# Attention's second pass in one run: the order of score products and value sums on TensorE, and eight modulation rows moved to later steps

## The chip, the cores and the metric

The kernel runs on one core of a Trainium2 chip. A core has five engines that run their own instruction streams in order: TensorE (PE in the profile, PEld its weight loads), VectorE (DVE), ScalarE (ACT), GpSimd (POOL) and SyncE (SP), which here issues all the DMAs. They wait for each other through semaphores. The metric is the device time of one execution in microseconds, lower is better.

## What is computed

One transformer block on 2048 tokens of 1024 channels, in float32: an attention with 32 heads in 4 segments of 512 tokens (a causal softmax inside the segment, plus a memory `M`, `z` that is carried from segment to segment), then a token-mixing MLP. Both are modulated by six rows that come from `silu(c) @ w_mod`.

```python
mod = (_silu(c) @ w_mod).reshape(c.shape[0], 6, 1, -1)
sa, ca, ga, sb, cb, gb = (mod[:, 0], mod[:, 1], mod[:, 2], mod[:, 3], mod[:, 4], mod[:, 5])
h = _layernorm(x, axis=-1) * (1 + ca) + sa
x = x + ga * _A_ref(h, A_wq, A_wk, A_wv, A_wo, A_beta)
h = _layernorm(x, axis=-1) * (1 + cb) + sb
x = x + gb * _B_ref(h, B_w1, B_b1, B_w2, B_b2)
...
logits = jnp.einsum("bhqd,bhkd->bhqk", qs, ks) * scale + mask
p = _softmax(logits, axis=-1)
a_dot = jnp.einsum("bhqk,bhkd->bhqd", p, vs)
o = g * a_mem + (1.0 - g) * a_dot
```

The two parts of it that matter here are `p` and `p @ vs` for one head of one segment, and `ga`, the row that scales the attention's result.

## The kernel before

**Stages.** A start normalises the first segment and makes the first modulation rows. The attention follows as a loop over 128 steps, then the product with `wo` (line 791), the second norm, and the MLP (line 921, more than half of the time), which the change leaves alone.

**Steps.** The heads are handled in 8 groups of 4, the segments in two passes: the first pass does segments 0 and 1 for all 8 groups, the second segments 2 and 3. `t` (0 to 31) counts (pass, group, segment), and step `n = 4 t + h` is one head of one segment. Steps 64 to 127 are the second pass. In round `n` the loop emits `scores` of step `n`, `maxima` of step `n + 3`, `values` of step `n - 2` (`VL = 2`), `project` pieces for a later `t`, and whatever was planned for that round.

**scores** (tiles `a`, lines 515 to 523) makes the transposed logits of a head in three PSUM banks. The causal triangle leaves 512 + 384 + 384 columns. The third bank takes two products: 128 columns (line 521) and then 256 (line 522). The operands are 32-bit tiles `sk`. ACT takes the exponential of each bank into `p` (lines 516, 519, 523), POOL masks the diagonal blocks (526), ACT makes the 16-bit high part `ph` (528), and POOL the 16-bit low part `p` in two halves of 640 columns (530).

**values** (tile `pv`, line 544) makes the weighted sums of a head with 20 products: 10 with the high part as weights and 97 columns of `vp`, then 10 with the low part and 65 columns. All add up in one PSUM bank. VectorE then divides and folds them (547, 549, 551). Below, these 20 products are called the sums. **maxima** makes the row maxima (products 478, VectorE 480), **project** the keys and values (192), queries (200) and transposes (405), **memory** the products 450 and 460 with VectorE lines 452 to 454 between them and the result `am`.

**Order.** The program is written round by round, but the instructions are put into each engine's stream by a list scheduler that weighs what is ready. So the pieces of one round are mixed with those of its neighbours. `tc.issue_after(i)` keeps what is written inside it behind instruction `i`; `behind(n, engines)` does this with the instructions that `scores` or `maxima` left in `marks` for round `n`.

**Modulation rows.** The last four of the six rows of `mod` are computed late on VectorE: 32 blocks `j` of 128 columns of `w_mod`. `mod_fetch(j)` (line 569) loads a block into a `raw` buffer, of which there are three, shared with the weight parts that pass 1 fetches, the token tiles and the `wo` blocks. `mod_late(j)` (line 573) multiplies and sums it. After block 7 the row `ga` is complete, is transposed on PE and written out; round 62 reads it back into `gaw`, and the `wo` blocks are scaled by it from round 66 on.

`mx` in lines 921 and 928 is the MLP's accumulator; `wv`, `wq` are weight parts that are split into two 32-bit parts (line 122); `wsp` and `hT` are scratch in DRAM, written in pass 1 and read in pass 2.

Of the kernel before, what the change touches and what calls it, by code (L numbers as in the profile page):

```python
# [18 lines left out]
P = 128  # L19
# [8 lines left out]
NV = 97  # L28
# [3 lines left out]
VL = 2  # L32
ML0 = 36
# [8 lines left out]
def attention_and_mlp(ctx, tc, x, wq, wkv, wo, beta, w1, b1, w2, b2, c, wm_a, wm_b, out):  # L42
    nc = tc.nc
    V, A, G, T, SY = nc.vector, nc.scalar, nc.gpsimd, nc.tensor, nc.sync
# [451 lines left out]
    marks = {}  # L496

    @contextmanager
    def behind(n, engines):

        with ExitStack() as s:
            for e in engines:
                if (n, e) in marks:
                    s.enter_context(tc.issue_after(marks[n, e].ins))
            yield

    def scores(t, h):
        d = st[t]
        n = 4 * t + h
        q, k = d["sk", h][:, 0], d["sk", h][:, 1]  # L510
        p32 = r_.tile([P, 1280], F32, tag="p32", bufs=3, name=f"p32_{t}_{h}")
        hi, lo = r_.tile([P, 1280], F16, tag="ph", bufs=3, name=f"ph{t}_{h}"), p32.bitcast(F16)[:, 0:1280]
        d["ph", h] = hi, lo
        b0 = bank("s2", 2, f"a0_{t}_{h}")
        T.matmul(b0, k[:, 0:128], q, start=True, stop=True)  # L515
        A.activation(p32[:, 0:512], b0, AF.Exp, scale=SCALE, bias=shift)  # L516
        b1_ = bank("s2", 2, f"a1_{t}_{h}")
        T.matmul(b1_[:, 0:384], k[:, 128:256], q[:, 128:512], start=True, stop=True)  # L518
        A.activation(p32[:, 512:896], b1_[:, 0:384], AF.Exp, scale=SCALE, bias=shift)
        b2_ = bank("s2", 2, f"a2_{t}_{h}")  # L520
        T.matmul(b2_[:, 0:128], k[:, 384:512], q[:, 384:512], start=True, stop=True)
        T.matmul(b2_[:, 128:384], k[:, 256:384], q[:, 256:512], start=True, stop=True)  # L522
        A.activation(p32[:, 896:1280], b2_[:, 0:384], AF.Exp, scale=SCALE, bias=shift)  # L523
        for base, step in ((0, 512), (896, 128)):
            w = bass.AP(tensor=p32.tensor, offset=p32.offset + base, ap=[p32.ap[0], [step, 2], [1, 128]])
            G.affine_select(w, w, pattern=[[0, 2], [1, 128]], compare_op=ALU.is_ge, fill=0.0, base=0,  # L526
                            channel_multiplier=-1)
        marks[n, "A"] = A.copy(hi, p32)  # L528
        for c in (slice(0, 640), slice(640, 1280)):
            marks[n, "G"] = G.tensor_tensor(lo[:, c], p32[:, c], hi[:, c], op=ALU.subtract)  # L530

    def values(t, h):
        pr, g, seg = its[t]
        d = st[t]
        am, ph = d["am"], d["ph", h]
        pv = bank("pv", 1, f"pv{t}_{h}").rearrange("p (a n) -> p a n", a=4)
        col = {0: lambda i: 128 * i, 1: lambda i: 512 + 128 * (i - 1), 2: lambda i: 1024 + 128 * (i - 2),
               3: lambda i: 896}
        n = 0
        for part, w in ((0, NV), (1, 65)):  # L540
            for i in range(4):
                for j in range(i + 1):
                    o = col[j](i)
                    T.matmul(pv[:, i, 0:w], ph[part][:, o:o + 128], d["vp"][:, j, h, 0:w], start=(n == 0),  # L544
                             stop=(n == 19), skip_group_check=True)
                    n += 1
        V.reciprocal(pv[:, :, 0], pv[:, :, 0])
        red = r_.tile([P, 4, 32], F32, tag="red", bufs=2, name=f"red{t}_{h}")
        V.tensor_reduce(red, pv[:, :, 1:97].rearrange("p a (c e) -> p a e c", c=3), axis=AX.X, op=ALU.add)
        ah = am[:, :, 32 * h:32 * h + 32]  # L550
        V.scalar_tensor_tensor(red if seg else ah, red, gate[:, 1, 4 * g + h:4 * g + h + 1],
                               pv[:, :, 0:1].to_broadcast([P, 4, 32]), op0=ALU.mult, op1=ALU.mult)
        if seg:
            G.tensor_tensor(ah, ah, red, op=ALU.add)
        if h < 3:
            return
        ps = bank("ms", 1, f"ops{t}")
        for i in range(4):
            T.transpose(ps[:, 128 * i:128 * i + 128], am[:, i], ident)
        ot = r_.tile([P, L], F32, tag="ot", bufs=1, name=f"ot{t}")  # L560
        A.copy(ot, ps)
        SY.dma_start(oT[g, :, L * seg:L * seg + L], ot)
        del st[t]
# [3 lines left out]
    def mod_fetch(j):  # L567
        r = a.tile([P, D], F32, tag="raw", bufs=3, name=f"rawm{j}")
        SY.dma_start(r, wm_b[P * j:P * j + P])
        return r  # L570

    def mod_late(j, r):
        V.scalar_tensor_tensor(r, r, 1.0, scb, op0=ALU.mult, op1=ALU.mult, accum_out=mcol[:, j:j + 1])
        if j == 7:
            mod_rows(0, 8)
        if j == 31:
            V.tensor_scalar_add(mcol[:, 16:24], mcol[:, 16:24], 1.0)
            mod_rows(8, 32)
# [14 lines left out]
    def at(f, n):  # L593
        if 0 <= n < 4 * NI:
            f(n // 4, n % 4)
# [25 lines left out]
    parts = (("v", 0), ("v", 1), ("q", 0))  # L621
# [36 lines left out]
    def later(n, fetch, m, f, engines):  # L658

        got = []  # L660
        plan(n, lambda: got.append(fetch()))
        plan(m, lambda: f(got[0]), engines)
# [13 lines left out]
                  n + n1, lambda r, g=g, kind=kind, part=part: split_part(g, kind, part, r), "A")  # L676
        plan(n + 4, lambda g=g: keep_w(g))
    for j in range(32):
        n = ML0 + 2 * j + (8 if j >= 8 else 0)
        later(n, lambda j=j: mod_fetch(j), n + (2 if j < 8 else 1), lambda r, j=j: mod_late(j, r), "V")  # L680
    plan(WO0 - 3, lambda: spread(gaw, 0))
    for i in range(8):
        n = WO0 + WOS * i
# [2 lines left out]
    for n in range(-LEADS, 4 * NI + VL):  # L686
        at(scores, n)
        at(maxima, n + LEADS)
        at(values, n - VL)
        m = n + LEADP  # L690
        if 0 <= m + 4 < 4 * NI:
            t = (m + 4) // 4
            if its[t][:2] not in W:
                with tc.issue_after(last_sk[t - 2 if t > 16 else 0, 3].ins):
                    load_w(its[t][1], its[t][0])
        if m >= 8:
            at(project, m)
        if 59 <= m < 67:
            seg, ct = 2 + (m - 59) // 4, 2 * ((m - 59) % 4)
            with ExitStack() as s:  # L700
                if seg == 3:
                    s.enter_context(tc.issue_after((last_sk[15, 3] if ct < 4 else last_nt[14, 3]).ins))
                reload_h(seg, ct)
                reload_h(seg, ct + 1)
        if 4 * NI - 5 <= m < 4 * NI + 3:
            i = m - 4 * NI + 5
            for c in (2 * (i % 4), 2 * (i % 4) + 1):
                wop[c, i // 4] = new_page(f"wo{c}_{i // 4}")
                if c < 5 or i < 4:
                    SY.dma_start(wop[c, i // 4].bitcast(F32), wos[c, i // 4])  # L710
        for f, engines in todo.pop(n, ()):
            with behind(n, engines):
                f()
# [427 lines left out]
```

## Time and profile before

| | |
|---|---|
| three runs | 2225.91, 2229.25, 2231.14 us; median 2229.25 us |
| the profiled execution | 2226.6 us, of which the span from first to last instruction is 2224.9 us |
| PE | busy 2190.3 us (98%), 13786 matmuls |
| DVE, ACT, POOL | busy 1666.7, 1135.7, 725.8 us (75%, 51%, 33%) |
| TensorE clock | 0.997 of full speed in the mean |

The profile's times are those of the profiled execution, so sums are made against 2226.6 us. A PE that is 98% busy leaves little idle time to win, but "busy" counts a matmul from its start to its modelled end, and matmuls overlap. How long a product holds the engine is read from the distance between starts, in the timeline. Step 0 of the attention starts at 98 us, step 64 at 564 us, and the last sums end near 1025 us.

### The profile page before, as it was taken

Reading aid. Unit: us, or ns where it says so; the run is one execution under the profiler, and the core shown is the slowest. Engines: PE = TensorE matmul, PEld = TensorE weight load, DVE = VectorE, ACT = ScalarE, POOL = GpSimd, SP = SyncE. Lnnn points to the kernel's source line nnn. Section 1 sums busy time; section 2 is a strip of 40 time slices with the busy share of each in tenths; the row PEclk is TensorE's granted clock in tenths of the full one; section 3 lists DMA queues with packets and bytes.
Section 4 is the critical chain, followed back from the end, with each engine's and each line's share of the span. In section 5 each row is a group of like instructions: output and inputs, shape, how many; then the busy total and the mean of one; then the engine's idle time right before and its main releaser. Section 6 shows DMA issues by size and latency. Waiting matters only on the chain.

```text
span 2224.9 us, 38052 instructions
## 1 busy us (share of the span) xinstructions
PE 2190.3 (98%) x13786; PEld 1881.0 (85%) x13786; DVE 1666.7 (75%) x3762; ACT 1135.7 (51%) x2050; POOL 725.8 (33%) x831
## 2 busy tenths in 40 slices
PE   8999999999999999999999999999999999999999
PEld 5988898888999999888888888888888888888887
DVE  7676777756777777664858766888888886969687
ACT  5486776756666666654636533533334242424232
POOL 2175766646767776663002200033330000000000
PEclk9999999999999999999999999999999999999999
DMA  7666666686556666664754687655556542414134
GB/s 287 192 187 191 175 181 193 189 279 216 170 180 205 188 183 211 193 219 143 231 194 186 226 304 275 243 223 220 204 202 219 206 148 64 145 57 147 57 123 151
DMA packets 175183, 423.03 MB, mean 190 GB/s; under 512 B 17524, under 2 KB 71828, under 8 KB 166036
## 3 DMA queue, kind: packets, MB, share of 16 engines
q1 hardware_dynamic: 174996, 420.61, 57.5%
q8 instruction: 109, 1.79, 0.3%
q14 instruction: 78, 0.64, 0.1%
HBM read 244.62 MB, written 125.06 MB: 166 GB/s over the span
## 4 chain that ended last, share of the span: by engine, by line
PE 87%; DVE 5%; DMA 3%; ACT 2%; POOL 1%; issue 1%; SPq 0%; DVEq 0%; ACTq 0%
PE mx L921 48%; PE nps L192 11%; PE po L791 8%; PE qps L200 7%; PE pv L544 3%; PE a L515 1%; PE sz L478 1%; PE sx L478 1%; DMA sk<-nt 1%; PE up L460 1%; PE a L518 1%; POOL p L530 1%; PE a L522 1%; PE sy L478 1%; PE rd L450 1%
## 5 line engine op out<-in xcount | busy, mean ns | idle before, releaser
L921 PE MATMUL mx<-bU,sp 128*128 128x512 f32 x2352 | 534.3, 389 | 0.9 <-DVE ac L928 0.9
L921 PEld LDWEIGHTS mx<-bU,sp 128*128 128x128 f32 x2352 | 441.3, 188 | 93.4 <-issue 1.3
L119 ACT CAST sp<-wr 128x384 fp32r<-128x384 f32 (+2 forms) x408 | 218.1, 547 | 431.8 <-PE mx L921 349.1
L192 PE MATMUL nps<-wv,h 128*128 128x256 f32 x3072 | 431.2, 283 | 1.6 <-DVE h L122 0.7
L921 PE MATMUL mx<-bA,sp 128*128 128x512 f32 x1764 | 430.5, 389 | 0.0
L530 POOL TENSOR_TENSOR p<-p,ph 128x640 f16<-128x640 f32 x256 | 380.2, 1485 | 138.5 <-ACT ph L528 134.5
L192 PEld LDWEIGHTS nps<-wv,h 128*128 128x128 f32 x3072 | 400.3, 189 | 9.4 <-DVE h L122 2.0
L921 PEld LDWEIGHTS mx<-bA,sp 128*128 128x128 f32 x1764 | 331.2, 188 | 68.7
L122 DVE TENSOR_TENSOR sp<-wr,sp 128x384 fp32r<-128x384 f32 (+2 forms) x408 | 259.8, 648 | 24.7 <-ACT sp L119 24.4
L928 DVE TENSOR_TENSOR ac<-mx,ac 128x512 f32<-128x512 f32 x280 | 189.9, 687 | 85.2 <-PE mx L921 84.1
L200 PE MATMUL qps<-h,wq 128*128 128x512 f32 x768 | 197.9, 400 | 0.0
L528 ACT CAST ph<-p 128x1280 f16<-128x1280 f32 x128 | 161.4, 1261 | 59.7 <-POOL p L526 59.6
L791 PE MATMUL po<-wo,ots 128*128 128x512 f32 x768 | 180.9, 391 | 0.0
L791 PEld LDWEIGHTS po<-wo,ots 128*128 128x128 f32 x768 | 142.7, 188 | 28.7
L200 PEld LDWEIGHTS qps<-h,wq 128*128 128x128 f32 x768 | 141.6, 190 | 27.7
L921 PE MATMUL mx<-bB,sp 128*128 128x512 f32 x588 | 164.0, 389 | 0.0
L526 POOL TENSOR_SCALAR_AFFINE_SELECT p<-p 128x256 f32<-128x256 f32 x256 | 134.1, 529 | 81.8 <-ACT p L523 53.9
L921 PEld LDWEIGHTS mx<-bB,sp 128*128 128x128 f32 x588 | 110.4, 188 | 22.9
L480 DVE CUSTOM_DVE_ANT_0 sz<-sz,mask 128x512 f32<-128x512 f32 x128 | 89.1, 696 | 52.0 <-PE sz L478 49.5
L480 DVE CUSTOM_DVE_ANT_0 sx<-sx,mask 128x128 f32<-128x128 f32 (+1 forms) x256 | 93.7, 366 | 44.1 <-PE sx L478 37.9
L928 DVE TENSOR_TENSOR cc<-mx,cc 128x512 f32<-128x512 f32 x140 | 94.9, 684 | 37.6 <-PE mx L921 37.4
L516 ACT ACTIVATE p<-a,shift 128x512 f32<-128x512 f32 x128 | 88.4, 691 | 41.2 <-PE a L515 40.4
(209 smaller groups left out, 3244.7 us busy)
## 6 DMA issues: line engine op xcount, KB each, us to landing
sk<-sg SPq DMA_DIRECT2D x384, 128.0 KB
wr<-in_w_dram SPq DMA_DIRECT2D x28, 1024.0 KB
wr<-in_w_dram SPq DMA_DIRECT2D x32, 768.0 KB
bstu<-ucd SPq DMA_DIRECT2D x28, 768.0 KB
wsp<-wv SPq DMA_DIRECT2D x32, 512.0 KB
rawm<-in_wm_b_dram SPq DMA_DIRECT2D x32, 512.0 KB
wv<-wsp SPq DMA_DIRECT2D x32, 512.0 KB
pcd<-cc SPq DMA_DIRECT2D x14, 1024.0 KB
```

The costliest lines, as they stand in the source:

```text
L119: last_hi[0] = A.copy(hi, src)
L122: return lo_eng.tensor_tensor(lo, src, hi.bitcast(F32), op=ALU.subtract)
L192: T.matmul(ps[:, aa], h[:, j, 128 * tt:128 * tt + 128], wt[:, i, o:o + 256], start=(n == 0), stop=(n >= 6 * NK - 2), skip_group_check=True)
L200: T.matmul(ps, wt[:, i, o:o + 128], h[:, j], start=(k + n == 0), stop=(3 * k + n == 3 * NK - 1))
L480: marks[4 * t + h - LEADS, "V"] = V.tensor_tensor_reduce(o, o, mask[:, 384 - 128 * i:], 1.0, -3.0e38, op0=ALU.add, op1=ALU.max, accum_out= ...
L516: A.activation(p32[:, 0:512], b0, AF.Exp, scale=SCALE, bias=shift)
L526: G.affine_select(w, w, pattern=[[0, 2], [1, 128]], compare_op=ALU.is_ge, fill=0.0, base=0, channel_multiplier=-1)
L528: marks[n, "A"] = A.copy(hi, p32)
L530: marks[n, "G"] = G.tensor_tensor(lo[:, c], p32[:, c], hi[:, c], op=ALU.subtract)
L791: T.matmul(ps, os_[:, i, P * ct:P * ct + P], wop[ct, nh][:, j], start=(n == 0), stop=(n == 3 * NK - 1))
L921: T.matmul(ps, ops[q][:, i, P * k:P * k + P], b[:, j], start=(m == 0 and first), stop=(m == 3 * nk - 1), skip_group_check=True)
L928: V.tensor_tensor(d, ps, d, op=ALU.add)
```

## The change

Four edits. In `scores` the third bank's two products change places, 256 columns first, and both now set `marks[n, "P"]`, so the mark is the 128-column one. In `values`, in the second pass only, the sums run in reverse: the low part first, and in each part the last block of rows first. In the loop, for steps of the second pass, `values` of step `n - 2` stands behind the mark of step `n`, so behind the last score product of that round. The first eight modulation blocks are fetched in rounds 49 to 56 and used one round later; before, they were fetched in rounds 36, 38, ... 50 and used two rounds later. Blocks 8 to 31 keep their rounds.

```diff
         b2_ = bank("s2", 2, f"a2_{t}_{h}")
-        T.matmul(b2_[:, 0:128], k[:, 384:512], q[:, 384:512], start=True, stop=True)
-        T.matmul(b2_[:, 128:384], k[:, 256:384], q[:, 256:512], start=True, stop=True)
+        for lo_, hi_, kt in ((128, 384, 2), (0, 128, 3)):
+            marks[n, "P"] = T.matmul(b2_[:, lo_:hi_], k[:, 128 * kt:128 * kt + 128], q[:, 128 * kt:], start=True,
+                                     stop=True)
         A.activation(p32[:, 896:1280], b2_[:, 0:384], AF.Exp, scale=SCALE, bias=shift)
...
-        for part, w in ((0, NV), (1, 65)):
-            for i in range(4):
-                for j in range(i + 1):
-                    o = col[j](i)
-                    T.matmul(pv[:, i, 0:w], ph[part][:, o:o + 128], d["vp"][:, j, h, 0:w], start=(n == 0),
-                             stop=(n == 19), skip_group_check=True)
-                    n += 1
+        order = [(i, j) for i in range(4) for j in range(i + 1)]
+        parts = [(0, NV), (1, 65)]
+        if pr:
+            order.reverse()
+            parts.reverse()
+        for part, w in parts:
+            for i, j in order:
+                o = col[j](i)
+                T.matmul(pv[:, i, 0:w], ph[part][:, o:o + 128], d["vp"][:, j, h, 0:w], start=(n == 0),
+                         stop=(n == 19), skip_group_check=True)
+                n += 1
...
     for j in range(32):
-        n = ML0 + 2 * j + (8 if j >= 8 else 0)
-        later(n, lambda j=j: mod_fetch(j), n + (2 if j < 8 else 1), lambda r, j=j: mod_late(j, r), "V")
+        n = 49 + j if j < 8 else ML0 + 2 * j + 8
+        later(n, lambda j=j: mod_fetch(j), n + 1, lambda r, j=j: mod_late(j, r), "V")
...
         at(maxima, n + LEADS)
-        at(values, n - VL)
+        with behind(n, "P" if n - VL >= 64 else ""):
+            at(values, n - VL)
```

What this does to PE's stream in the second pass is seen at the sums of step 94. In the rows, `a` is a score product, `pv` a sum, `LDWEIGHTS` the sum's weights (`ph` the high part, `p` the low part), `nps` a product of `project`. Before, a stretch of PE's stream around the first score product of step 96:

```order
L544 MATMUL pv_2_11936<-vp_10975,ph_2_11701 128x97
L515 MATMUL a_24_0_11900<-sk_0_497 128x512
L544 LDWEIGHTS ph_2_11701
L544 MATMUL pv_2_11936<-vp_10975,ph_2_11701 128x97
L192 MATMUL nps_1_12090<-wv_5_0_1_11519,h_3_7064 128x256
L544 LDWEIGHTS p_23_2_11700
L544 MATMUL pv_2_11936<-vp_10975,p_23_2_11700 128x65
```

The sums of one head stood in pieces, with 32-bit products of 512 and 256 columns between them. Now, the same sums begin here:

```order
L478 MATMUL sy_1_12164<-sk_1_502 128x384
L405 MATMUL kps_12207<-ident,k_26_11962 128x128 x2
L522 MATMUL a_24_0_11906<-sk_0_497 128x256
L522 MATMUL a_24_0_11906<-sk_0_497 128x128
L549 LDWEIGHTS p_23_2_11700
L549 MATMUL pv_2_11936<-vp_10975,p_23_2_11700 128x65
```

They moved behind the third bank of step 96, low part first, and 17 of the 20 now follow one another. From step 64's first score product on, PE's stream had 155 separate pieces of sums before and has 85 now.

On VectorE the place to see is around round 48, between the two halves of `memory` for `t = 13`. `rd`, `rdd` and `am` belong to `memory` (lines 452 to 454), `rawm` is a modulation block, `wq` a weight part that is split, `pv` and `red` the folding of a head's sums, `sx` and `mx` the maxima. Before:

```order
L454 TENSOR_TENSOR am_6473<-rd_0_6474,rdd_0_6477 128x256
L480 ISA sx_1_6760,mx_0_6646<-sx_1_6760,mask 128x256
L480 ISA mx_0_6646 128x1
L573 SCALAR_TENSOR_TENSOR rawm_6406,mcol<-rawm_6406,scb 128x1024
L122 TENSOR_TENSOR wq_7_0_0_6496<-rawq_0_6279,wq_7_0_0_6496 128x512
L122 TENSOR_TENSOR wq_7_0_1_6499<-rawq_0_6279,wq_7_0_1_6499 128x512
L452 TENSOR_SCALAR rdd_1_6484<-rd_1_6481 128x8
L547 RECIPROCAL pv_2_6546<-pv_2_6546 128x4
L453 RECIPROCAL rdd_1_6484<-rdd_1_6484 128x8
L549 TENSOR_REDUCE red_2_6568<-pv_2_6546 128x128
L454 TENSOR_TENSOR am_6473<-rd_1_6481,rdd_1_6484 128x256
```

The second half of `memory` stood behind modulation block 5 and a weight part. Now:

```order
L480 ISA sx_1_6742,mx_0_6626<-sx_1_6742,mask 128x256
L480 ISA mx_0_6626 128x1
L452 TENSOR_SCALAR rdd_1_6467<-rd_1_6464 128x8
L453 RECIPROCAL rdd_1_6467<-rdd_1_6467 128x8
L454 TENSOR_TENSOR am_6456<-rd_1_6464,rdd_1_6467 128x256
L552 RECIPROCAL pv_2_6529<-pv_2_6529 128x4
L122 TENSOR_TENSOR wq_7_0_0_6479<-rawq_0_6265,wq_7_0_0_6479 128x512
```

The block is gone from there, and the weight part moved behind `am`. The first modulation block now stands in VectorE's stream after the maxima of step 53, the last of the eight after those of step 60; before, they stood after those of steps 41 to 55.

## The prediction

> **What bounds the kernel now.** First the page's head and the busy time by stage (columns after the stretch: its length, then busy us and instruction count of PE, PEld, DVE, ACT, POOL, then granted TensorE clock, DMA share, GB/s).
>
> ```profile
> span 2224.9 us, 38052 instructions
> PE 2190.3 (98%) x13786; PEld 1881.0 (85%) x13786; DVE 1666.7 (75%) x3762; ACT 1135.7 (51%) x2050; POOL 725.8 (33%) x831
> ...
> 98.00:446.00 348.00, 338.90 (x3012) 309.69 (x3011) 260.28 (x749) 258.97 (x479) 225.69 (x253) 1.00 0.63 181
> 446.00:512.00 66.00, 61.84 (x512) 56.53 (x511) 40.26 (x122) 36.11 (x65) 33.91 (x44) 0.92 0.82 259
> 512.00:564.00 52.00, 50.45 (x466) 46.32 (x466) 32.22 (x101) 33.87 (x59) 33.22 (x42) 1.00 0.66 209
> 564.00:1025.00 461.00, 456.40 (x3967) 412.56 (x3966) 328.47 (x1001) 292.83 (x505) 312.73 (x373) 1.00 0.63 192
> ```
>
> PE sets the pace. In the second pass, where most of the change lies, PE is busy 456.4 of 461 us, so taking waits away there can win 4.6 us at most; a larger gain must make the products themselves hold PE for less. The stretch 446 to 512 us stands out: its clock is 0.92 and PE loses 4.2 us. PE's waits there and in the second pass, and the chain that ended last through that place:
>
> ```profile
> PE up L460 <- DVE am L454: 3.8, 3, 3.5
> ...
> PE a L515 <- DMA sk<-nt: 2.5, 3, 1.4
> PE pv L544 <- DVE red L551: 0.9, 2, 0.8
> PE pv L544 <- POOL p L530: 0.3, 1, 0.3
> ...
> 444.88 4.51 DMA rawm<-in_wm_b_dram
> 451.44 2.61 DVE wq L122 x2
> 454.82 0.34 DVE am L454
> 455.29 2.10 PE up L460 x8
> ...
> 455.29 2.10 PE L460 MATMUL up<-v,pk 128*128 128x132 f32 x8 [3.48 <-DVE am L454]
> ...
> 451.00:455.30 4.30, 0.82 (x6) 0.49 (x4) 4.30 (x10) 2.68 (x6) 2.51 (x2) 0.83 1.01 357
> 455.30:464.10 8.80, 8.80 (x46) 7.87 (x47) 6.33 (x20) 4.41 (x9) 4.43 (x9) 0.50 0.98 370
> ```
>
> The first row is the largest of PE's waits in 98 to 564 us, the next three are of the second pass. The chain says why PE stood still for 3.48 us: a modulation block was 4.51 us on its way, VectorE waited for it, then did it and a weight part, and only then `am`, for which PE's `up` products waited. Behind that the clock is 0.50 for 8.8 us.
>
> **Part 1: fewer returns from sums to 32-bit products.** The timeline gives start, length, then the instruction; what a product costs is the distance to the next start.
>
> ```profile
> 644.86 0.26 PE L544 MATMUL pv<-vp,ph 128*128 128x97 bf16 x2
> 644.94 0.47 PE L478 MATMUL sz<-sk 96*128 96x512 f32 x1
> 645.26 0.35 PE L544 MATMUL pv<-vp,ph 128*128 128x97 bf16 x4
> 645.43 0.42 PE L518 MATMUL a<-sk 98*128 98x384 f32 x1
> 645.69 0.35 PE L544 MATMUL pv<-vp,ph 128*128 128x97 bf16 x4
> ...
> 651.02 0.34 PE L518 MATMUL a<-sk 98*128 98x384 f32 x1
> 651.20 1.20 PE L192 MATMUL nps<-wv,h 128*128 128x256 f32 x9
> 652.23 0.40 PE L478 MATMUL sz<-sk 96*128 96x512 f32 x1
> 652.47 0.52 PE L192 MATMUL nps<-wv,h 128*128 128x256 f32 x3
> 652.83 0.40 PE L478 MATMUL sx<-sk 96*128 96x128 f32 x2
> ```
>
> A 512-column product takes 0.24 us between 32-bit products (652.23 to 652.47) and 0.32 behind a sum (644.94 to 645.26); a 384-column one 0.18 (651.02 to 651.20) and 0.26 (645.43 to 645.69). So each return from the sums to such a product costs 0.08 us, while four sums in a piece take 0.17 (645.26 to 645.43), 0.04 each, as if nothing had been cut. I counted in PE's order the pieces of sums that are followed by one of these products (lines 192, 200, 478, 515 to 522, 791): in the second pass 121 before and 52 now, in the first pass, where the scheduler's choices shift a little, 105 and 111. That is 63 fewer: 63 x 0.08 = 5.0 us. All of it is on the path, since PE has no other slack. Bounds: 0, if only the recorded starts shift and not the work; 6.3, if a return costs 0.1.
>
> [...] The rows decide for 0.08.
>
> **Part 2: the 128-column product last, with sums behind it.**
>
> ```profile
> 640.48 0.22 PE L521 MATMUL a<-sk 98*128 98x128 f32 x1
> 640.54 0.34 PE L522 MATMUL a<-sk 98*128 98x256 f32 x1
> 640.72 0.40 PE L478 MATMUL sx<-sk 96*128 96x128 f32 x2
> ...
> 525.39 0.22 PE L478 MATMUL sx<-sk 96*128 96x128 f32 x1
> 525.45 0.39 PE L544 MATMUL pv<-vp,ph 128*128 128x97 bf16 x5
> 525.66 0.48 PE L515 MATMUL a<-sk 98*128 98x512 f32 x1
> ```
>
> The pair takes 0.06 + 0.18 = 0.24 us, though 256 columns alone take 0.12 (three in 652.47 to 652.83): a 128-column product with a 32-bit one behind it costs 0.12, twice its 0.06. The one place where a 128-column product has a sum behind it shows 0.06, and its five sums then take the usual 0.04 each (525.45 to 525.66). In the new order 49 of the 128 third banks have a sum directly behind the 128-column product: 49 x 0.055 = 2.7 us. Where a 32-bit product follows instead, the swap gives nothing. Bounds: 0, since one place is little evidence, and 3.
>
> **Part 3: the modulation blocks leave rounds 36 to 52.** At the 3.48 us stall VectorE's order now has `am` ahead of the weight part and no block. What goes is the 3.48 us and the half clock behind it, 8.8 x 0.5 = 4.4: together 7.9 us. What is late next there is the weight load that the projection needs, which has the products in front as cover. Bounds: 0 (another stall of the kind) to 7.9.
>
> The eight blocks and their loads now queue on VectorE and SP after step 53's maxima, in front of the folding of sums and the next maxima, and wait for a DMA that starts one round ahead, not two.
>
> ```profile
> L573 DVE SCALAR_TENSOR_TENSOR rawm<-rawm,scb 128x1024 f32<-128x1024 f32 x32 | 49.5, 1548 | 8.4 <-DMA rawm<-in_wm_b_dram 8.2
> ```
>
> A block is 1.55 us, so eight are 12.4 us, where VectorE has 26 us free in 446 to 512 and 20 in 512 to 564. Blocks 11 to 31 already run one round behind their loads in the second pass, and no wait of PE there names them. I take 0; were one exposed with a DMA as late as in the chain, it is 3.5 us once, with the clock's loss 7.9.
>
> **Part 4: new waits of the sums.** They now begin with the low part, which POOL ends last, and stand behind the third bank, so less can be fitted in between. A tight place, step 79:
>
> ```profile
> 687.42 2.37 POOL L530 TENSOR_TENSOR p<-p,ph 128x640 f16<-128x640 f32 x1
> ...
> 688.85 0.60 PE L544 MATMUL pv<-vp,ph 128*128 128x97 bf16 x10 [0.15 <-DVE red L551]
> 689.29 0.28 PE L544 MATMUL pv<-vp,p 128*128 128x65 bf16 x4
> 689.84 0.36 PE L544 MATMUL pv<-vp,p 128*128 128x65 bf16 x6 [0.27 <-POOL p L530]
> ```
>
> The low part is done at 689.79. High part first, PE waited 0.27 us; low part first it would wait from 688.85, 0.94: 0.67 us more. POOL is busy 313 of 461 us, so this is not the rule. I take three such places, 2.0 us. Bounds: 0, and 0.3 x 62 steps = 19.
>
> The rest of the order shifts everywhere, in the first pass too, where PE loses 9.1 us in 98 to 446 us. That can go either way: I take 0, within a third of it, 3.
>
> **The sum.** 2226.6 (the profiled execution) - 5.0 - 2.7 - 7.9 + 0 + 2.0 = 2213.0. The median of the three runs, 2229.25, is 2.65 above the profiled one, so 2215.6 against it. A measurement of this kernel tells about 0.2% from no change, 4.5 us: faster is below 2224.8, slower above 2233.7.
>
> **The rivals.**
>
> [...]
>
> *The stall moves.* Only parts 1, 2 and 4 remain: 2226.6 - 7.7 + 2.0 + 2.65 = 2223.6. For it: the DMA share is 0.82 in 446 to 512 us, where the first of the moved blocks are loaded. Against: PE's order has more projection products between `rd` and `up` now. How much of it returns hangs on the clock:
>
> ```profile
> 128.00:133.00 5.00, 3.57 (x17) 2.41 (x17) 4.66 (x16) 5.00 (x10) 3.12 (x7) 1.00 1.02 255
> 133.00:136.40 3.40, 3.40 (x23) 3.19 (x23) 2.76 (x3) 3.40 (x8) 3.13 (x3) 0.50 1.00 260
> ```
>
> Here PE was busy 3.57 of 5 us in pieces, and the clock was halved for 3.4 us, a loss of 1.7. So scattered waits of 1.4 us are enough for a second price. [...]
>
> *The sums wait for POOL (slower).* If the low part is late in most of the 62 steps, part 4 grows. At 0.35 us per step it is 21.7 instead of 2.0: 2235.3. It decides from 0.32 us per step, where the sum passes 2233.7. For it: the low part comes first and nothing is left to fit in where the order puts sums right behind the bank, as at step 94. Against: POOL's 0.3 us in the list of waits, one in 461 us.
>
> *The gain does not come*: parts 1 and 2 at their lower bounds and the stall elsewhere, 2226.6 + 2.0 + 2.65 = 2231.3, no change.
>
> **Chances and range.** Forecast 0.66; order does not matter 0.06; stall moves 0.14; POOL 0.08; no gain 0.06. The two middle cases centre 1.3 us inside the faster bound, so two thirds of them count as faster: 0.66 + 0.13 = 0.79 faster; 0.07 + 0.06 = 0.13 same; 0.08 slower. The low end is parts 1 and 2 at their upper bounds, no new waits and 3 us less elsewhere: 2229.25 - 6.3 - 3 - 7.9 - 3 = 2209.0, and lower if further waits of the first pass fall away, for which I take 2206. The high end takes in the two middle cases with 3 us from the rest of the order: 2227.
>
> **What would show it.** Right: the 0.50 clock at 455 us and the wait of `up` for `am` are gone; a 384-column product behind a sum still takes 0.26 us but there are half as many; 128 columns with a sum behind take 0.06; the second pass is about 5 us shorter after its new waits, 461 to 456. Wrong: PE's waits for `p` of line 530 beyond 6 us in the second pass, a new stretch with the clock at 0.50, or a second pass as long as before with no more waits.

## The result, and the profile after

The changed kernel took 2224.22 us in the median of 18 runs (2217.13 to 2226.59), the kernel before 2227.66 us in 18 runs on the same chip (2224.23 to 2233.23). The medians are 3.4 us apart, the means 5.8. The ratio of the runs is 0.9974, with a 95% interval of 0.9964 to 0.9984, so the gain is 3.6 to 8.0 us for these two programs. It was forecast as 13.6. The profiled execution took 2224.45 us.

The head of the profile after and its busy time by stage, in the same columns and stretches as before; the last row is a place that the text comes to:

```profile
span 2222.7 us, 38130 instructions
PE 2184.5 (98%) x13786; PEld 1881.3 (85%) x13786; DVE 1673.2 (75%) x3762; ACT 1132.7 (51%) x2050; POOL 723.6 (33%) x831
...
98.00:446.00 348.00, 338.16 (x3006) 308.41 (x3005) 254.38 (x742) 258.09 (x479) 219.45 (x253) 1.00 0.60 173
446.00:512.00 66.00, 61.04 (x513) 55.40 (x512) 44.88 (x118) 37.45 (x66) 37.34 (x44) 0.95 0.87 278
512.00:564.00 52.00, 50.98 (x464) 46.83 (x464) 38.61 (x121) 31.37 (x57) 32.02 (x40) 1.00 0.71 234
564.00:1025.00 461.00, 454.66 (x3988) 418.13 (x3987) 327.08 (x991) 292.19 (x504) 313.59 (x373) 1.00 0.63 192
...
494.50:501.30 6.80, 6.20 (x31) 5.94 (x32) 3.10 (x11) 4.05 (x7) 4.83 (x7) 0.50 0.93 336
```

The second pass fits 21 more products into the same 461 us (3988 for 3967), and PE is idle in it for 6.3 us where it was for 4.6. In 446 to 512 us the idle time went up from 4.2 to 5.0 us: the stretch that was to be cleared isn't. PE's waits, first of 446 to 564 us, then of the second pass, the largest of each:

```profile
PE pv L549 <- POOL p L531: 2.3, 2, 1.4
PE sx L478 <- DMA sk<-sg: 1.5, 1, 1.5
PE sz L478 <- DVE rdd L452: 1.0, 1, 1.0
...
PE po L797 <- ACT ots L119: 1.4, 1, 1.4
PE kps L405 <- ACT k L398: 1.3, 1, 1.3
PE sx L478 <- DMA sk<-sg: 1.1, 1, 1.1
PE pv L549 <- POOL p L531: 0.9, 1, 0.9
PE nmps L486 <- DVE am L454: 0.7, 1, 0.7
PE rd L450 <- DVE am L454: 0.6, 1, 0.6
```

The 3.5 us wait of `up` for `am` is gone. In its place stand several of 1.0 to 1.5 us for other things. The chain that ended last, at 484 to 496 us (in part):

```profile
484.08 1.03 SPq L375
...
485.84 0.66 SPq L493
...
487.89 1.58 DMA sk<-nt
489.49 0.59 ACT sg L119
490.07 1.17 ACT ph L529
491.31 1.41 POOL p L531
492.79 2.27 POOL p L531
495.10 0.51 PE pv L549 x6
```

SP issues the transfers of one stack after another (lines 375 and 493). Just ahead of this stack stands the load of a moved modulation block, one of the eight blocks of the row `ga` that the change moves, in SP's timeline:

```profile
482.75 0.58 SPq L574 DMA_DIRECT2D rawm<-in_wm_b_dram  x1
```

The last row maxima land late, ACT's copy `sg` waits for them, the exponential's high part `ph` stands behind that copy on ACT, POOL makes the low part from `ph`, and the sums wait for it. Behind this PE runs at half clock for 6.8 us (the last row of the first fence). Whether the block's load is what made the row maxima late, this chain doesn't show; the experiments come back to it.

**What a product costs** is as the prediction read it. PE's timeline in the second pass:

```profile
710.52 0.34 PE L522 MATMUL a<-sk 98*128 98x256 f32 x2
710.70 0.30 PE L549 MATMUL pv<-vp,p 128*128 128x65 bf16 x4
...
711.55 0.60 PE L549 MATMUL pv<-vp,ph 128*128 128x97 bf16 x10
711.97 0.49 PE L515 MATMUL a<-sk 98*128 98x512 f32 x1
712.29 0.40 PE L192 MATMUL nps<-wv,h 128*128 128x256 f32 x2
```

The pair of 256 and 128 columns with a sum behind it now takes 0.18 us (710.52 to 710.70), not 0.24. A 512-column product behind a sum still takes 0.32 (711.97 to 712.29).

**Where the time went.** For this I priced each kernel's order on PE by the distances between starts that its trace shows between like products: 0.229 us for 512 columns, 0.176 for 384, 0.113 for 256, 0.060 for 128, 0.0435 and 0.029 for the sums of 97 and 65 columns. A product of the kinds counted in part 1 is charged as if it started no sooner than 0.115 after the start of what is ahead of it. In the records it starts 0.03 behind a sum and then holds PE for 0.32 instead of 0.23; the two together are the same. The first sum of a piece takes 0.017 more. The sum over a pass is its *product time*. What the pass took beyond that is its *lost time*: waits, half clock, and the error of the prices. The first pass goes from the 512-column score product of step 0 to that of step 64, the second from there to product 8700, early in the product with `wo`.

| us, profiled execution | first pass: product + lost | second pass: product + lost | both |
|---|---|---|---|
| before | 432.4 + 33.4 | 491.4 + 11.0 | 968.2 |
| after | 433.5 + 34.6 | 480.6 + 16.8 | 965.5 |

So the products give back 9.7 us, more than the 7.7 forecast, and the lost time takes 7.0 of it, 5.8 in the second pass. What stands behind product 8700, the rest of the product with `wo` and the MLP, takes nearly the same in both (1154.2 and 1154.7 us to the start of the last product).

Three limits of the table. The price list is a model, and a difference in lost time of a microsecond or two means nothing: with only the prices above, and no others for the transposes and `memory`, every kernel's lost time comes out some 5 us higher in the second pass, while the differences stay. The two passes don't hold quite the same work: the scheduler moved 13 products of 256 columns and a few others across the border, 1.7 us, from the second pass to the first, so the second pass's own saving is 9.1 us, not 10.8. And the lost time is that of one execution. Of the rise of 5.8 us in the second pass, PE's named waits in 564 to 1030 us explain 3.0 (4.6 us in all before, 7.6 after); the rest has no name in the profile.

### The profile page after: what moved, and what is told of

It reads as the page before. It is cut to its first block, busy times and chain, and to the rows that moved or that the text cites. A ratio compares the mean times of both kernels' runs of the same rounds, so it can differ in the third digit from the quotient of the medians.

```text
span 2222.7 us, 38130 instructions
## 1 busy us (share of the span) xinstructions
PE 2184.5 (98%) x13786; PEld 1881.3 (85%) x13786; DVE 1673.2 (75%) x3762; ACT 1132.7 (51%) x2050; POOL 723.6 (33%) x831
## 4 chain that ended last, share of the span: by engine, by line
PE 82%; DVE 6%; DMA 5%; ACT 3%; issue 1%; POOL 1%; SPq 1%; DVEq 0%; ACTq 0%
PE mx L927 47%; PE nps L192 10%; PE qps L200 7%; PE po L797 6%; PE pv L549 3%; DMA otr<-oT 1%; PE a L515 1%; DMA sk<-sg 1%; PE sz L478 1%; PE sx L478 1%; POOL p L531 1%; PE a L522 1%; PE sy L478 1%; PE a L518 1%; PE up L460 1%
```

## The experiments

**One edit alone, or left out.** Four kernels. *mods_old* is after with the modulation blocks in their old rounds, *mods_only* is before with the moved blocks alone:

```diff
-        n = 49 + j if j < 8 else ML0 + 2 * j + 8
-        later(n, lambda j=j: mod_fetch(j), n + 1, lambda r, j=j: mod_late(j, r), "V")
+        n = ML0 + 2 * j + (8 if j >= 8 else 0)
+        later(n, lambda j=j: mod_fetch(j), n + (2 if j < 8 else 1), lambda r, j=j: mod_late(j, r), "V")
```

(mods_only has the same two lines the other way round.) *mods_early* is after with `n = 4 * j + 2` for the first eight blocks, and *high_first* leaves out the two reversals in `values`:

```diff
-        if pr:
-            order.reverse()
-            parts.reverse()
```

Expected of mods_old:

> The changed kernel with the first eight modulation blocks back in their old rounds 36 to 52. Theory A (the order of the products saves 8 to 10 us of TensorE time, and the saving is lost again to stalls near round 50 and to new waits in the second pass): PE's order has 55 fewer returns from sums to 32-bit products than before and 49 third banks with sums behind, 8.5 us less product time; the second pass is 5 us shorter than before as in the changed kernel, and the stall at 450 us with the half clock is back, so 2222 us, the same as the changed kernel within 3. Theory B (moving the blocks is what gained, the order of products gains nothing): 2227 to 2228, as before.

Of mods_only:

> The kernel before with only the modulation blocks moved to rounds 49 to 57. Theory A: the stall is not removed but found again 40 us later behind the same busy DMA queue, and PE's order has as many returns as before, so 2225 to 2230, no change. Theory B: all of the gain of the changed kernel, 2224. The prediction's part 3 would say 2220.

Of high_first:

> The changed kernel with the sums of the second pass again high part first and first block first; they still stand behind the third bank. Theory A says the new waits of the second pass for POOL's low part (0.9 us in the changed kernel's list) and their like go, and the runs end on 65 columns (0.015 us more per return, 0.7 us together): 2222 to 2225, about as the changed kernel. If the low part first is what lost the second pass's 6 us, 2218 to 2220.

Of mods_early:

> The changed kernel with the first eight modulation blocks fetched in rounds 2, 6, ... 30 and used one round later, away from rounds 36 to 60. Theory A with the DMA queue as the cause of the moved stall: the loads no longer stand in the queue ahead of the stacked keys and queries at 440 to 495 us, no wait over 2 us and no half clock there, 2216 to 2219. If the stall of that stretch comes from the second pass's weights and pages alone, it stays and the time is that of the changed kernel, 2224.

| us | median | ratio to before, 95% | first pass | second pass |
|---|---|---|---|---|
| mods_old | 2227.39 | 0.9994 [0.9986, 1.0003] | 433.6 + 33.3 | 481.5 + 17.6 |
| mods_only | 2229.47 | 1.0000 [0.9990, 1.0010] | 434.3 + 28.4 | 490.2 + 17.8 |
| high_first | 2224.74 | 0.9983 [0.9973, 0.9992] | 433.5 + 33.0 | 481.3 + 18.6 |
| mods_early | 2223.83 | 0.9981 [0.9973, 0.9990] | 433.8 + 32.3 | 481.6 + 16.8 |

The moved blocks are worth nothing alone and about 3 us inside after (2227.39 to 2224.22), against 7.9 forecast; the draws below show that 3 us can be chance. By its time mods_old came out as theory B had it, by its product time, 9.9 us less in the second pass, as theory A had it. mods_early took its loads away from the tight stretch and did clear it, but came out at 2223.83, where 2216 to 2219 had been expected of that.

The four also tell where the stall of before went. mods_old has the blocks in their old rounds, and PE's wait of `up` for `am` isn't in its list. The largest in 440 to 530 us is another one:

```profile
PE a L515 <- DMA sk<-nt: 2.0, 1, 2.0
```

In mods_only, where the blocks alone moved, that wait is down to 0.3 us. So either edit was enough to remove the stall, the one to the products too, which changes the scheduler's order in the first pass. The half clock between 490 and 500 us doesn't follow the blocks either. The rows of that stretch in mods_old (blocks in their old rounds), no_swap (described below, blocks moved as in after) and mods_early (blocks fetched long before):

```profile
490.00:500.00 10.00, 7.77 (x46) 5.90 (x44) 2.93 (x12) 3.83 (x7) 3.51 (x4) 0.95 0.98 342
490.00:500.00 10.00, 9.46 (x92) 8.37 (x90) 9.12 (x23) 7.24 (x14) 7.16 (x9) 1.00 1.02 330
490.00:500.00 10.00, 10.00 (x72) 8.60 (x71) 4.38 (x15) 6.07 (x10) 3.95 (x5) 1.00 0.64 177
```

The first runs at a lower clock for a while (0.95 in this row, 0.88 in the next ten microseconds), and the second, with the moved loads, does not (1.00). That the load ahead of the stack caused the late maxima in after is therefore not shown.

And the second pass loses 17 to 19 us in all four. High part first does not bring that down, so beginning with the low part is not what the new waits come from, as far as one order tells. mods_only does not touch the products of the second pass and yet loses 6.8 us more in it than before. That raised a suspicion against the order of before: that its 11.0 us were luck.

**The price of a cut, by itself.** Both kernels add 784 products of 16 bits and 65 columns to the first half of the MLP, into a PSUM bank that nobody reads: *dummy_pieces* one behind every three products of `mx`, *dummy_run* four behind every twelve. The scheduler joins some, so that they stand in 440 and in 148 pieces.

```diff
+        dm = bank("pv", 1, "dm")
...
-                    T.matmul(ps, ops[q][:, i, P * k:P * k + P], b[:, j], start=(m == 0 and first),
+                    mm = T.matmul(ps, ops[q][:, i, P * k:P * k + P], b[:, j], start=(m == 0 and first),
...
+                for c in range(1 if nk == 4 else 0):            # dummy_run: 4 * (k == 3)
+                    with tc.issue_after(mm.ins):
+                        mm = T.matmul(dm[:, 0:65], ops[q][:, 0, 0:64].bitcast(F16),
+                                      ops[q][:, 1, 0:64].bitcast(BF16)[:, 0:65], start=True, stop=True,
+                                      skip_group_check=True)
```

> The changed kernel with 784 added products of a 16-bit weight and 65 columns in the first half of the MLP, where PE is the bound; they write a PSUM bank that nothing reads. One stands behind each group of three 512-column products: PE's order has 440 pieces of them. If a return from such a product to a 32-bit one costs 0.086 us and an entry 0.017: 784 x 0.029 + 440 x 0.103 = 68 us more than the changed kernel. If only the recorded starts shift: 784 x 0.029 = 23 us more.

> The same 784 added products, four in a run behind each twelve 512-column products: 148 runs in PE's order. If a return costs 0.086 and an entry 0.017: 784 x 0.029 + 148 x 0.103 = 38 us more than the changed kernel, 30 less than with the pieces. If the order of products does not matter to TensorE: 23 us more, the same as with the pieces.

dummy_pieces took 2300.49 us (ratio 1.0328 [1.0306, 1.0350]), dummy_run 2263.58 (1.0162 [1.0141, 1.0184]), each in two runs: 76 and 39 us more than after, where 68 and 38 were expected. The heads of their profiles:

```profile
span 2298.1 us, 39698 instructions
PE 2259.2 (98%) x14570; PEld 1868.1 (81%) x14570; DVE 1658.2 (72%) x3762; ACT 1133.4 (49%) x2050; POOL 716.1 (31%) x831
```

```profile
span 2262.7 us, 39696 instructions
PE 2224.1 (98%) x14570; PEld 1890.8 (84%) x14570; DVE 1665.8 (74%) x3762; ACT 1131.2 (50%) x2050; POOL 713.8 (32%) x831
```

The same 14570 products differ by 36.9 us for 292 more pieces: 0.126 us a piece. A part of that lies outside the MLP, where the added products don't stand. From the first to the last product of `mx` the two traces take 1142.4 and 1110.1 us, 0.11 us a piece. A piece in dummy_pieces, with three products behind it:

```profile
1300.00 0.20 PE L933 MATMUL dm<-sp 128*128 128x65 bf16 x1
1300.04 0.94 PE L928 MATMUL mx<-bB,sp 128*128 128x512 f32 x3
1300.81 0.20 PE L933 MATMUL dm<-sp 128*128 128x65 bf16 x1
```

So the cut is real time, not a shift of recorded starts, and the case that the order of products does not matter, 0.06 in the forecast, is out. The price is above the 0.08 of the prediction because a piece costs at its entry too. In medians of this trace the product behind a piece holds PE for 0.314 us instead of 0.227, which is the return; the product ahead of it takes 0.012 more, and a single added product 0.039 instead of 0.029.

**The edits in other shares.** *no_swap* puts the 128-column product back in front of the 256-column one. *behind_all* holds the sums behind the scores, and reverses them, in the first pass too:

```diff
-        if pr:
+        if True:
...
-        with behind(n, "P" if n - VL >= 64 else ""):
+        with behind(n, "P"):
```

> The changed kernel with the third bank's products in the old order, 128 columns first, and the mark on the 256-column one. PE's order keeps the runs of sums but no 128-column product has sums behind it: 49 x 0.055 = 2.7 us more product time and a few returns more, 3.6 us in all, 2226 to 2229. If the place of the 128-column product does not matter, 2224.

> The changed kernel with the sums of the first pass too behind the third bank and in reverse. PE's order has 126 + 49 - 55 - 49 = 56 fewer returns and 72 fewer pieces than the changed kernel: 8.0 us less product time by the counted prices. Theory A: as much of it is lost to new waits as in the second pass (9.7 saved, 5.8 lost), more in the first pass, where DVE and POOL are fuller: 2220 to 2224. If waits eat all of it, 2224 to 2228.

| us | median | ratio to before, 95% | first pass | second pass |
|---|---|---|---|---|
| no_swap | 2224.20 | 0.9984 [0.9972, 0.9996] | 434.3 + 27.8 | 483.7 + 17.7 |
| behind_all | 2235.94 | 1.0044 [1.0028, 1.0061] | 428.3 + 46.7 | 477.9 + 21.7 |

In no_swap the products cost 3.9 us more than in after over both passes, 3.1 of it in the second; 3.6 was expected, 2.7 of it for part 2. But its first pass lost 6.8 us less, and the time is that of after. behind_all shows the loss most clearly. Over both passes it has 7.9 us less product time than after, as expected (8.0), but its time, 2235.94, is far outside the 2220 to 2228 that either theory gave. Its first pass has 5.2 us less product time than after's and 12.1 more lost time; its 46.7 is also more than any other order lost in the first pass, 39 at most. PE's largest waits in the first pass and its busy time, of behind_all:

```profile
PE sz L478 <- DVE mx L480: 6.9, 6, 2.9
PE a L515 <- DMA sk<-nt: 4.3, 3, 2.1
PE sx L478 <- DMA sk<-sg: 2.5, 3, 1.2
PE a L522 <- ACT p L516: 1.6, 4, 1.0
...
98.00:446.00 348.00, 332.88 (x2955) 304.71 (x2954) 248.59 (x731) 256.57 (x475) 217.21 (x248) 0.99 0.59 171
```

The largest waits are not those of the sums for POOL. They are of the maxima for their banks, and of the scores and maxima for the rows that the DMAs bring: work that waits in other orders too. That spread sums, ready long before, had covered it is the reading that fits; the list itself can't show it. PE is idle for 15.1 of 348 us, in after 9.8. Of the two engines that were expected to be fuller in the first pass, only DVE is: in after it is busy for 73% of 98 to 564 us and 71% of 564 to 1025, POOL for 62 and 68%.

**Draws of the order.** To see how much an order is worth by chance, one number that has nothing to do with the sums was moved by one round, in before and in after alike: the start of the `wo` blocks, or the rounds of the modulation blocks from the ninth on.

```diff
-WO0 = 65
+WO0 = 66                # or 64
...
-        ... ML0 + 2 * j + 8
+        ... ML0 + 2 * j + 9      # or 7
```

In before (b_) the first two were expected to show that its low waits were luck; the pairs (a_ with b_) came from what they gave. *early_ns* is mods_early with no_swap.

> The kernel before with one number changed: the preparation of the eight output-weight blocks begins at round 66 instead of 65 (WO0). It does the same work; its first pass is the same instruction for instruction, its second pass is drawn again by the scheduler, with 93 returns from 65-column sums where before has 81, and 174 pieces of sums for 155, which by the step between products is +1.2 us. If the order of before was a lucky draw (the first theory: any edit redraws the list and loses the low waits of its second pass), the second pass has waits of 15 to 19 us where before has 11, and the time is 2231 to 2236 us. If the larger waits of after come from the edits themselves (the second theory), the second pass keeps waits of 10 to 13 us, and the time is 2227 to 2230 us.

> The kernel before with the modulation blocks from the ninth on one round later (ML0 + 2 j + 9 for ML0 + 2 j + 8); the same work. Returns from 65-column sums in the second pass 95 for 81, +1.0 us. Lucky draw: second-pass waits 15 to 19 us and 2230 to 2236 us. Waits tied to the edits: second-pass waits 10 to 13 us and 2227 to 2230 us.

> The kernel after with the same one number changed (WO0 66). The returns stay as in after (4 from 65-column sums, 50 from 97-column ones in the second pass). Lucky draw: after is an ordinary draw already, so another draw is as good: second-pass waits 14 to 20 us, 2220 to 2228 us. Waits tied to the edits: second-pass waits as in after within 1 us (16 to 18), 2223 to 2226 us.

> The kernel after with the first eight modulation blocks at rounds 4 j + 2 (away from the reload of the pages at rounds 51 to 58) and with the 128-column product back in its old place, first in the third bank; sums of the second pass behind the scores as in after. If the two savings seen apart add up (no waits drawn anew), 2222 to 2224 us; if each order is a draw of its own, anywhere from 2219 to 2229 us. The sums' part alone stays in every case: the second pass's product time is 482 to 485 us where before has 491.4.

> The kernel before with the output-weight blocks one round earlier (WO0 64 for 65); the same work. Returns in the second pass 86 for 81 and 170 pieces for 155, +0.8 us of product time. Systematic theory (orders with the sums spread as fillers have fewer waits in the second pass, whatever the draw): second-pass waits 9 to 16 us. Draw theory (waits have nothing to do with where the sums stand, each order draws from one distribution of 10 to 26): as likely above 16.5 as below. Time 2227 to 2233 us.

> The kernel before with the modulation blocks from the ninth on one round earlier (ML0 + 2 j + 7); the same work. Product time +0.5 us. Systematic theory: second-pass waits 9 to 16 us. Draw theory: as likely above 16.5 as below. Time 2227 to 2234 us.

> The kernel after with WO0 64. Product time of the second pass 480 to 482 us in every case. Systematic theory: second-pass waits 16.5 to 26 us, 2223 to 2233 us. Draw theory: as likely below 16.5 as above, 2216 to 2233 us.

> The kernel after with the modulation blocks from the ninth on one round later. Product time of the second pass 480 to 482 us. Systematic theory: second-pass waits 16.5 to 26 us, 2223 to 2233 us. Draw theory: as likely below 16.5 as above, 2216 to 2233 us.

> The kernel after with the modulation blocks from the ninth on one round earlier (ML0 + 2 j + 7), the partner of the kernel before with the same edit (2234.5 us). Product time of the second pass 480 to 482 us in every case. Systematic theory (held sums cost some 5 us of waits and save some 10 us of product time, the draw spreads this by 5 us): 4 to 5 us below its partner, 2224 to 2236 us, waits 17 to 26 us. If the edits are worth only what this one order happens to wait, it is as likely above its partner as below.

| us | before so shifted: median, ratio | second pass | after so shifted: median, ratio | second pass |
|---|---|---|---|---|
| no shift | 2227.66, 1 | 491.4 + 11.0 | 2224.22, 0.9974 [0.9964, 0.9984] | 480.6 + 16.8 |
| WO0 = 66 | 2229.21, 1.0000 [0.9989, 1.0010] | 492.7 + 9.9 | 2232.54, 1.0012 [1.0003, 1.0021] | 480.7 + 26.1 |
| WO0 = 64 | 2238.42, 1.0046 [1.0029, 1.0062] | 492.6 + 19.2 | 2235.26, 1.0028 [1.0012, 1.0044] | 480.5 + 24.0 |
| blocks + 9 | 2236.84, 1.0031 [1.0016, 1.0046] | 493.5 + 15.4 | 2227.37, 0.9995 [0.9985, 1.0006] | 480.8 + 21.2 |
| blocks + 7 | 2234.54, 1.0032 [1.0016, 1.0047] | 493.1 + 17.7 | 2228.45, 0.9997 [0.9988, 1.0006] | 479.0 + 20.7 |

early_ns took 2236.71 us (1.0031 [1.0020, 1.0042]; second pass 483.5 + 23.2), above all the times that were expected of it (2219 to 2229), with the product time where it was expected: two variants that were each as good as after are 12 us worse together.

A number that only moves the same work by one round is worth up to 11 us. The product time hardly takes part in that: in the second pass it is 10.8 to 14.1 us lower after the change, in all five pairs. Between 1.7 and 5.0 of this is work handed to the first pass, and over both passes it is 9.5 to 10.9 lower. The lost time of the second pass is higher after the change in all five, by 3.0 to 16.2 us, 7.1 in the mean.

Pure luck of before, which I had put first, would have taken b_wo66 to 15 us or more; it has 9.9, but b_late9, with 15.4, came out as luck would have it. The opposite, that waits are tied to the edits alone, fell too: a_wo66 was to have 16 to 18 and has 26.1, and b_wo64 and b_late7, with 19.2 and 17.7, lie above the 9 to 16 that spread sums were to cost whatever the draw. The times of a_wo66, b_wo64 and a_wo64 lie 2 to 5 us above everything expected of them, those of b_late9 and b_late7 just above. What the pairs suggest is both: a part that comes with the edits, 7.1 us with a 95% interval of 0.7 to 13.6, and a spread of some 5 us from the draw.

Which edit the first part belongs to is not settled by the pairs, for the two kernels of a pair differ in all four edits. mods_only holds no sums and moves the blocks, and it loses 17.8 us; mods_old holds the sums and leaves the blocks, and it loses 17.6. Also, each lost time is that of one execution. Most of the profiled ones are within 3.3 us of their kernel's median, but that of b_late7 is 6.8 us slower than its median and that of a_wo64 10.3 faster.

The times themselves rest on many runs. Over the five pairs the ratios differ by 0.26, -0.12, 0.18, 0.36 and 0.35% in favour of after, 0.21% in the mean, with a 95% interval of about 0.25% to either side. What the edits are worth apart from their draw is therefore some 4.6 us, and not told from nothing with certainty.

**Between the two.** *no_behind* has the reversed order but does not hold the sums behind the scores:

```diff
-        with behind(n, "P" if n - VL >= 64 else ""):
+        with behind(n, ""):
```

> The kernel after with the sums of the second pass in the reversed order but not held behind the scores: pieces of sums 127 (after 85, before 155), returns from 65-column sums 20 (after 4, before 81). Product time of the second pass 483 to 485 us. Systematic theory: some fillers are back, so waits between the classes, 14 to 19 us, and 2220 to 2232 us with the draw's spread. Draw theory: waits anywhere from 10 to 26 us.

It took 2224.79 us (ratio 0.9986 [0.9974, 0.9997]); the second pass is 484.2 + 14.7, with 127 pieces of sums where before has 155 and after 85. It gave back 3.6 us of after's product time and won 2.1 of the lost time, and comes out where after does. That is the way that the theory of lost cover says, but 2.1 us is within what the price list can be off, and the draw alone could give as much.

No variant beat after beyond the uncertainty; the best, mods_early, stands 0.4 us below it.

## Why the prediction was wrong

The forecast was faster, and it is; but 3.4 us by the medians, 5.8 by the means, where 13.6 were forecast. In the profiled executions the two passes became 2.7 us shorter: 9.7 less product time, 7.0 more lost. Against the forecast, part 3 is off by 9.1 us, part 4 by 3.8, and parts 1 and 2 by 2.0 the other way.

- **Part 1 and part 2 held, and were too small.** Together 7.7 us were forecast, 9.7 came. By the price list part 1 is 6.7 for its 5.0, and part 2 is 3.1 for its 2.7. The size that was off is the price of a cut: 0.08 was only its return, and the 63 pieces fewer save their entries too, 1.1 us. The rest is in the returns: 77 fewer are behind 65-column sums, which cost 0.086, and 14 more behind 97-column ones at 0.0715. By the added-product kernels, at 0.11 us a piece, the 63 pieces would be 6.9. Had the order of products not mattered (the 0.06 in the forecast: parts 1 and 2 at 0, so 2223.4 us), the added products would have cost the same in both kernels; the 36.9 us between them (32.2 inside the MLP's products) disagree.
- **Part 3 failed, and it is the step that carried most of the miss.** The stall at 455 us and its half clock did go, but the wait is gone in mods_old too, where the blocks stayed, so it did not take the moved blocks to remove it. The prediction's own sign of being wrong, a new stretch with the clock at 0.50, came at 494.5 us. The step that was wrong is "what is late next there is the weight load", with products in front as cover. What was late next, at 490 us, was the next stack of keys: transfers one after another on SP, the copy `sg` and the high part behind them on ACT, the low part on POOL, the sums. The first pass was to become 7.9 us shorter; instead its lost time rose by 1.2. In mods_only the blocks alone took 5.0 us off the first pass's lost time, and the second pass's rose by 6.8, for a ratio of 1.0000. Of the rivals, "the stall moves" describes it, with its 2223.6 us against 2224.2; that the sum comes out there is in part chance, since parts 1, 2 and 4 were all off as well.
- **Part 4 had the wrong cause and was too small.** 2.0 us of waits for POOL were forecast; the second pass lost 5.8 more. The profile after names POOL's low part for 0.9 us of PE's waits there, and high part first left 18.6 us lost, so the low part is not the bulk of it. What fits is that the held sums lost their use as cover: behind_all shows other waits that come up, and all five pairs have more lost time after the change. But mods_only loses as much with no sum held, so this cause is argued and not shown. The prediction had the words, "less can be fitted in between", and priced only the wait for the low part.
- **The rest of the order, 0 within 3, was much too narrow.** The five orders of before lie between 2227.7 and 2238.4 us, the five of after between 2224.2 and 2235.3, in each set by one number.
- **The second pass's own forecast, about 5 us shorter (461 to 456), came out**: 502.4 to 497.4 us to product 8700. That is luck: too little product time saved and too little lost time were forecast, and the two errors cancel.

Not settled: how much of the 5.8 us in this one order is lost cover, how much the moved blocks, and how much draw. The pairs say 7.1 in the mean for all four edits together, from 3.0 to 16.2.

## What to carry to other kernels

On an engine that is nearly always busy, small products that are ready early may be worth something as cover, which is argued here and not shown. So two sums belong to a change that gathers them: what the cuts cost (here 0.11 us a piece, of which the distance behind a sum shows 0.08), and the waits that the pieces may have covered, for which one should look through the waits of the neighbouring work and not only through those of the moved one. Taking one stall out of a list that a scheduler orders need not gain its length: here the 3.48 us wait and its half clock went, and the first pass lost 1.2 us more. And a stall that one order has may be gone with another edit, as in mods_old. Where an order is drawn by a scheduler, move an unrelated number by one and measure that first: here it is worth up to 11 us, more than the change.

## What the runs showed that was not expected

- A 16-bit product of 65 columns put between 32-bit ones costs 0.11 us for the piece beyond its own length (32.2 us for 292 pieces inside the MLP, 36.9 in the kernels' times), about four times the 0.029 that one takes inside a run.
- The clock is not the same in every execution of the same program. The ten runs of a_wo64 lie between 2224.92 and 2242.69 us. Its profiled one is the fastest, with a mean clock of 1.000; the other nine have means of 0.995 to 0.998 and 2231.4 us or more. The rows on span and clock of that run and of before:

```profile
core 0: 2223.2 us, clock 1.000
```

```profile
core 0: 2224.9 us, clock 0.997
```

  One profile can miss the lower clock. A mean clock of 0.995 to 0.998 over 2235 us is, as an estimate from these means, 4 to 11 us lost to the clock, of the 6 to 18 us by which the nine are slower; why that one execution kept its clock, no run shows. The 18 runs of after fall into two groups too, seven at 2217 to 2222 us and eleven at 2223.6 to 2226.6.
- The half clock from 494.5 us in after came amid waits of the sums of 0.4, 0.9 and 1.4 us, scattered ones like those ahead of the 1.7 us loss at 133 us before. The row of after for the five microseconds ahead of it, in which PE was busy for 2.92 us:

```profile
489.50:494.50 5.00, 2.92 (x24) 1.91 (x23) 3.69 (x7) 3.16 (x5) 3.11 (x2) 1.00 0.95 344
```

  That scattered waits of 1.4 us are enough for it, as the prediction has it, is not so everywhere. In these five microseconds of before PE was busy for 3.27 us, less than the 3.57 ahead of 133 us, and the clock stayed at 1.00 there and in the next ten:

```profile
385.00:390.00 5.00, 3.27 (x23) 2.69 (x24) 5.00 (x22) 0.84 (x2) 0.17 (x1) 1.00 1.01 346
390.00:400.00 10.00, 9.21 (x68) 7.73 (x66) 9.86 (x30) 8.71 (x20) 4.88 (x7) 1.00 0.55 175
```

  Nor was the clock halved behind the single wait of 1.5 us that ended at 479.5 us in after: it is 1.00 in 475 to 480 us and in the five behind them. What tells these places apart, no run shows.
